# A planned attention and GEGLU kernel: one lane rule holds SP's stores, turns and loads back by a microsecond in the plan

## The chip, the cores and the metric

The kernel runs on one core of one Trainium2 chip. The metric is the device time of one execution in microseconds, the median of several executions.

Engines go by the names of the profile: PE does matmuls and PEld its weight loads, DVE, ACT and POOL do vector, activation and general work, and SP issues most of the DMA transfers. SPq and ACTq are the DMA queues that SP and ACT issue to.

## The reference

The reference is a transformer block in float32 on one sequence of 2048 tokens with 640 features: a pre-normalised attention with 32 heads of 20 features, where each token sees itself and the 255 tokens before it, and a pre-normalised GEGLU layer with 1536 hidden features, both with a residual.

```python
def _A_ref(x, wqkv, wo):
    B, S, D = x.shape
    H = 32; Dh = D // H; W = 256
    qkv = (lambda x, *d: x.transpose(*d))((x @ wqkv).reshape(B, S, 3, H, Dh), 2, 0, 3, 1, 4)
    q, k, v = qkv[0], qkv[1], qkv[2]
    scores = jnp.einsum("bhqd,bhkd->bhqk", q, k) * (Dh ** -0.5)
    idx = jnp.arange(S)
    mask = (idx[:, None] - idx[None, :] >= 0) & (idx[:, None] - idx[None, :] < W)
    scores = jnp.where(mask[None, None], scores, -1e9)
    p = _softmax(scores, axis=-1)
    o = jnp.einsum("bhqk,bhkd->bhqd", p, v)
    return (lambda x, *d: x.transpose(*d))(o, 0, 2, 1, 3).reshape(B, S, D) @ wo
def _B_ref(x, w_gate, w_up, w_down):
    return (_gelu(x @ w_gate) * (x @ w_up)) @ w_down
x = A_x
h = x + _A_ref(_layernorm(x, axis=-1), A_wqkv, A_wo)
h2 = h + _B_ref(_layernorm(h, axis=-1), B_w_gate, B_w_up, B_w_down)
```

## The kernel before

**Tiling.** Tokens go in 16 blocks of 128, two of them to a chunk of 256, so attention has eight chunks, 0 to 7. Float32 numbers are split into two float16 parts, high and low (`xh` and `xl`, `oh` and `ol`, `w1h` and `w1l` and so on), and a product is the sum of three matmuls.

**The way of a chunk.** `x_lane` loads a block of x (`load_x`, tile `xt`), normalises it to `xp` and turns it with two transposing DMAs to `xh` and `xl`. `qk(c, which)` makes the queries (`which` 0) or keys (1) of chunk c on PE; `qk_out` copies each of three pieces to a tile `qks` and ACT's queue writes it to DRAM, `qk<-qks`. In the trace's names the DRAM tile of chunk 3 is `qk30` for queries and `qk31` for keys. `stack` reads them back in the layout that the scores want, six DMAs `qT<-qk` and six DMAs `kT<-qk` on SP's queue. When both are read, `maxima` computes score tiles `ra` and `rb` (`rb<-kT,qT`) whose row maxima DVE takes (`max_out`), and the maxima are written into spare rows of `qT`. Then come the scores for the softmax (`ra<-qT,kT`), the exponentials on ACT (`pt`), the mask on POOL, and the products with the values (`pv<-pt,v`). `wo_block` multiplies the attention's output of a block (`oh`, `ol`) by `wo`, DVE adds it to the residual in `ht` (`wo_out`), and SP stores `ht` to `h_dram`. The GEGLU layer works in chunks of four blocks, loads `ht` from `h_dram`, and has the stretch behind attention to itself.

**What sets the order.** The program writes out every engine's instructions one after another, and the engines run them in that order. A planner picks that order as the program is built. The class `Clock` keeps a modelled time for each engine, for each tile's last write and read, and for DMAs a window of eight: a DMA starts in the model not before the eighth DMA ahead of it, on SP's or ACT's queue alike, has landed. The built program has the same rule, with eight semaphores that the DMAs use in turn. Every piece of work is a generator that yields what its next step needs, an engine and a time at which its inputs are ready, and `Lane` wraps it. The main loop goes through the lanes in an order of precedence, lets the first one whose `start(now)` holds take one step, and moves `now` on by 0.03 us when none does. All instructions are issued by one helper, so all have line 199 in the profile.

`start` compares the inputs' ready time with `now`: a step may start when `self.need() <= now + 0.1`. Steps that need SP alone yield `("sync",)`: the block stores to `h_dram`, the loads and turns of x, the loads of `ht`, the loads, turns and partial sums of the GEGLU layer, and also the reads in `stack` and the weights' loads in `load_lane`. Reads in `stack` of chunks from 2 on carry a pace of their own, one DMA each time that the modelled DMA line is less than `PACE` = 1.0 us ahead:

```python
if c > 1:
    yield ("sync",), lambda: nc.moved["sync"] - PACE
nc.sync.dma_start(to[rows], ...)
```

Of the kernel before, what the change touches and what calls it, by code (L numbers as in the profile page):

```python
# [253 lines left out]
def block_kernel(ctx: ExitStack, tc: tile.TileContext, x, wqkv, wo, wg, wu, wd, out):  # L254
# [27 lines left out]
    def done(name):  # L282
# [19 lines left out]
    FFBACK = dict(split_lane=0.4, scale_lane=0.4, chunk_lane=0.3, token_sums=0.1,  # L302
                  sums_lane=0.2, norm_lane=0.2)
    EARLY = 0.6
    PACE = 1.0
    SWAY = 4

# [231 lines left out]
    def products(n, term, ready=None, at_=None):  # L539


        ps = [at_[0]] if at_ else []
        col = at_[1] if at_ else 0

        def start(i):
            if ready and not ready(i) or not ps and opened["mm"] >= banks["mm"]:
                return INF
            t = nc.ready([x for ab in term(i) for x in ab], "tensor")
            return t if ps else max(t, nc.slot(psums["mm"], "mm", banks["mm"]))

        for i in range(n):
            yield ("tensor",), lambda i=i: start(i)
            if not ps:
                ps.append(bank("mm"))
            m = term(i)
            for k, (l, r) in enumerate(m):
                if k:
                    yield pe()
                o = ps[0][:, col:col + r.free_size()]
                nc.tensor.matmul(o, l, r, start=(i == 0 and k == 0),  # L560
                                 stop=(i == n - 1 and k == len(m) - 1))
                pos["dense"] += r.free_size() * 3 // len(m)
        return o
# [203 lines left out]
    def stack(c, which, d):  # L767
# [10 lines left out]
        for par in range(2):  # L778
            for m, i in enumerate(((0, 0, 1), (0, 1, 0))[which]):
                rows = slice(64 * par + DH * m, 64 * par + DH * m + DH)  # L780
                if c > 1:
                    yield ("sync",), lambda: nc.moved["sync"] - PACE
                nc.sync.dma_start(to[rows], d.rearrange("(a d i) m n -> a m d i n", a=2,
# [774 lines left out]
    class Lane:  # L1558
# [11 lines left out]
        def start(self, now):  # L1570

            if "tensor" in self.engs:
                return nc.t["tensor"] <= now + AHEAD and self.need() <= max(now, nc.t["tensor"])
            name = self.gen.__name__
            back = self.back
            if name in ("split_lane", "scale_lane"):
                back = PREP if not W["o", 0].ready else FFPREP
            elif name == "x_lane":
                back = EARLY if not B[XF].full else LATE
            elif name == "max_out" and not W["v"].ready:  # L1580
                back = RAMPMAX
            if isinstance(self.engs, Soon):
                back = max(back, OUT)
            if ffpools[1]:
                back = FFBACK.get(name, OUT)
            return (all(nc.t[e] <= now + back for e in self.engs if e != "sync")
                    and self.need() <= now + 0.1)

    load_x(0)
    load_x(1)  # L1590
# [20 lines left out]
    now = 0.0  # L1611
# [85 lines left out]
```

## Time and profile before

| | |
|---|---|
| median of three executions | 1022.89 us (1022.6 to 1025.46) |
| the profiled execution | 1022.7 us |
| its span, first to last instruction | 1020.8 us |
| mean granted clock of PE | 0.998 |
| busy: PE, PEld | 998.5 us, 698.8 us |
| busy: DVE, ACT, POOL | 748.3 us, 437.9 us, 299.4 us |
| reads `kT<-qk` and `qT<-qk` | 48 DMAs each, 160 KB |
| writes `qk<-qks` | 32 DMAs of 256 KB, 16 of 128 KB |

Times are read from one profiled execution. A row of the timeline has the start, the length, the engine, the operation with its tiles, the count of instructions that are shown as one, and in brackets the idle time of the engine in front of it with what ended it. For a DMA issue the length is that of the issue on the queue, not of the transfer; a row "DMA" in the chain has the time from issue to landing. A row of the waits has the total, the number of waits and the longest. A row of the windows has the bounds, the length, the busy time and count of PE, PEld, DVE, ACT and POOL, the granted clock, the DMA share and GB/s.

### The profile page before, as it was taken

To read this page: it belongs to the slowest core of one execution; us is meant where nothing else is said; L and a number is where in the kernel's file an instruction comes from. 1 tells how busy PE (TensorE), PEld (TensorE's weight loads), DVE (VectorE), ACT (ScalarE), POOL (GpSimd) and SP (SyncE) were. 2 spreads that over 40 slices of the span, in tenths; PEclk is the share of its full clock that TensorE was granted. 3 is DMA by queue.
4 is the path that set the end of the run, shared out by engine and by line. 5 is a ranking of instruction groups with operands and counts; after the bars stand their busy time and mean duration, and the time that the engine had idled before them with its cause. 6 is when DMAs were issued, how large, how long until landed. Compare 5 with 4: busy or idle time off the path is not lost.

```text
span 1020.8 us, 30772 instructions
## 1 busy us (share of the span) xinstructions
PE 998.5 (98%) x12925; PEld 698.8 (68%) x12925; DVE 748.3 (73%) x2221; ACT 437.9 (43%) x706; POOL 299.4 (29%) x489
## 2 busy tenths in 40 slices
PE   8999999998999999999999999989999999999998
PEld 7876677675776766776655664567777777777776
DVE  6888999885776757675688787798996975544553
ACT  6514645664445654555557643522222222221220
POOL 7102224343333432333335511254313300000000
PEclk9999999999999999999999999999999999999999
DMA  8658686271460723315303433233553532222211
GB/s 306 135 116 172 190 167 169 75 132 55 95 140 20 121 75 85 75 45 106 131 29 105 84 126 103 78 129 106 154 181 90 162 137 78 78 97 85 78 53 52
DMA packets 105835, 112.68 MB, mean 110 GB/s; under 512 B 38368, under 2 KB 79584, under 8 KB 105696
## 3 DMA queue, kind: packets, MB, share of 16 engines
q1 hardware_dynamic: 93600, 99.97, 36.4%
q10 hardware_dynamic: 12096, 10.75, 3.4%
q8 instruction: 101, 1.65, 0.7%
q14 instruction: 38, 0.31, 0.1%
HBM read 73.73 MB, written 28.84 MB: 100 GB/s over the span
## 4 chain that ended last, share of the span: by engine, by line
PE 83%; DMA 7%; DVE 5%; issue 2%; ACT 2%; SPq 1%; POOL 0%; DVEq 0%; ACTq 0%; POOLq 0%
PE mm L199 43%; PE pv L199 12%; PE ra L199 12%; PE rb L199 10%; PE tp L199 7%; DMA kT<-qk 3%; DMA qk<-qks 2%; DVE junk L199 1%; SPq L199 1%; DMA qT<-qk 1%; ACT pt L199 1%; DVE am L199 0%; DVE w1l L199 0%; DVE ht L199 0%; DMA wsl<-in_wo_dram 0%
## 5 line engine op out<-in xcount | busy, mean ns | idle before, releaser
L199 POOL TENSOR_SCALAR_AFFINE_SELECT pt<-pt 128x512 f32<-128x512 f32 x352 | 176.7, 518 | 277.5 <-ACT pt L199 261.4
L199 DVE CUSTOM_DVE_ANT_0 junk<-rb,band 128x320 bf16<-128x320 f32 x224 | 109.5, 489 | 48.5 <-PE rb L199 43.3
L199 DVE CUSTOM_DVE_ANT_0 junk<-ra,band 128x320 bf16<-128x320 f32 x224 | 109.4, 489 | 38.9 <-PE ra L199 33.4
L199 ACT ACTIVATE pt<-rb,esc 128x640 f32<-128x640 f32 (+2 forms) x129 | 98.3, 769 | 81.2 <-PE rb L199 65.5
L199 ACT ACTIVATE pt<-ra,esc 128x640 f32<-128x640 f32 (+2 forms) x127 | 96.6, 767 | 75.0 <-PE ra L199 63.9
L199 PE MATMUL pv<-pt,v 128*21 128x128 f32 x2880 | 105.3, 276 | 0.3 <-POOL pt L199 0.2
L199 PEld LDWEIGHTS <-ah 128*128 128x128 f16 x768 | 75.1, 98 | 28.4 <-issue 1.2
L199 ACT ACTIVATE gel<-gel,ffk 128x512 f32<-128x512 f32 x36 | 26.0, 722 | 144.0 <-DVE gel L199 144.0
L199 PEld LDWEIGHTS pv<-pt,v 128*21 128x21 f32 x2880 | 68.8, 100 | 10.8 <-issue 1.0
L199 PEld LDWEIGHTS <-ws 128*128 128x128 f16 x720 | 70.4, 98 | 8.2
L199 PEld LDWEIGHTS <-qT 60*64 60x64 f16 x1280 | 30.4, 104 | 66.4 <-issue 53.1
L199 PEld LDWEIGHTS <-kT 62*64 62x64 f16 x2880 | 63.5, 107 | 11.6 <-issue 8.0
L199 PEld LDWEIGHTS <-gu 128*128 128x128 f16 x440 | 42.0, 98 | 36.1 <-issue 1.7
L199 DVE SCALAR_TENSOR_TENSOR ht<-mm,ffk,ht 128x320 f32<-128x320 f32 x96 | 52.2, 545 | 12.0 <-PE mm L199 10.0
L199 ACT CAST ah<-gel 128x512 f16<-128x512 f32 x48 | 29.7, 618 | 66.7 <-DVE gel L199 64.7
L199 PE MATMUL mm<-xh,w1h 128*128 128x256 f16 x200 | 54.7, 274 | 0.9 <-DVE qks L199 0.9
L199 PE MATMUL mm<-xl,w1h 128*128 128x256 f16 x200 | 54.7, 273 | 0.0
L199 PE MATMUL mm<-xh,w1l 128*128 128x256 f16 x200 | 54.7, 273 | 0.0
L199 PE MATMUL rb<-kT,qT 60*64 60x320 f16 (+4 forms) x636 | 41.2, 283 | 9.5 <-DMA kT<-qk 8.8
L199 PE MATMUL mm<-w3h,oh 128*128 128x320 f16 x160 | 48.2, 301 | 0.0
L199 PE MATMUL mm<-w3l,oh 128*128 128x320 f16 x160 | 48.2, 301 | 0.0
L199 PE MATMUL mm<-w3h,ol 128*128 128x320 f16 x160 | 48.2, 301 | 0.0
(299 smaller groups left out, 2522.5 us busy)
## 6 DMA issues: line engine op xcount, KB each, us to landing
ws<-wsums SPq DMA_DIRECT2D x24, 640.0 KB
qk<-qks ACTq DMA_DIRECT2D x32, 256.0 KB
qT<-qk SPq DMA_DIRECT2D x48, 160.0 KB
kT<-qk SPq DMA_DIRECT2D x48, 160.0 KB
wsums<-ws SPq DMA_DIRECT2D x12, 640.0 KB
ht<-in_x_dram SPq DMA_DIRECT2D x16, 320.0 KB
h_dram<-ht SPq DMA_DIRECT2D x16, 320.0 KB
ht<-h_dram SPq DMA_DIRECT2D x16, 320.0 KB
```

The lines of the kernel that those rows point to most:

```text
L199: r = real(*args, **kw)
```

## The change

A new number `HELD` = 1.0 us is subtracted where 0.1 us was added, for steps that need SP alone, apart from those of the generators `stack` and `load_lane`. Such a step may start when its inputs have been ready for 1.0 us in the plan, and not from 0.1 us before on.

```diff
     EARLY = 0.6
+    HELD = 1.0
     PACE = 1.0
...
+            late = 0.1 if self.engs != ("sync",) or name in ("stack", "load_lane") else -HELD
             return (all(nc.t[e] <= now + back for e in self.engs if e != "sync")
-                    and self.need() <= now + 0.1)
+                    and self.need() <= now + late)
```

The planner then writes another order. On SP's queue, at the reads of chunk 3 (`qT` and `kT` from `qk30` and `qk31`; `xh`, `xl` are turns of x; the number behind a tile's name only tells its allocations apart), before:

```order
L199 DMA h_dram_72<-ht_3109 128x640
L199 DMA qT_4213<-qk30_2547 20x16x256 x5
L199 DMA ht_4264<-in_x_dram 128x640
L199 DMA_TRANSPOSE xh_4272<-xp_3336 128x5x128
L199 DMA_TRANSPOSE xl_4273<-xp_3336 128x5x128
L199 DMA xt_4319<-in_x_dram 128x640
L199 DMA qT_4213<-qk30_2547 20x16x256
L199 DMA kT_124<-qk31_2930 20x16x256 x5
L199 DMA_TRANSPOSE xh_4272<-xp_4321 128x5x128
L199 DMA_TRANSPOSE xl_4273<-xp_4321 128x5x128
L199 DMA xt_4629<-in_x_dram 128x640
L199 DMA kT_124<-qk31_2930 20x16x256
```

One turn stood between the fifth and the sixth query read, and another between the fifth and the sixth key read. The same place now:

```order
L199 DMA h_dram_72<-ht_2935 128x640
L199 DMA qT_4181<-qk30_2542 20x16x256 x6
L199 DMA kT_124<-qk31_3082 20x16x256 x3
L199 DMA_TRANSPOSE xh_4328<-xp_3170 128x5x128
L199 DMA_TRANSPOSE xl_4329<-xp_3170 128x5x128
L199 DMA xt_4401<-in_x_dram 128x640
L199 DMA kT_124<-qk31_3082 20x16x256 x3
L199 DMA ht_4523<-in_x_dram 128x640
L199 DMA_TRANSPOSE xh_4328<-xp_4403 128x5x128
L199 DMA_TRANSPOSE xl_4329<-xp_4403 128x5x128
L199 DMA xt_4651<-in_x_dram 128x640
```

The first turn has moved behind the third key read, and the second behind all twelve reads.

On SP's queue, at the reads of chunk 7 (`qk70`, `qk71`), where `ht_8519` is block 10's residual and `ht_9075` block 11's, before:

```order
L199 DMA h_dram_72<-ht_8519 128x640
L199 DMA qT_10094<-qk70_8927 20x16x256 x3
L199 DMA ht_10170<-in_x_dram 128x640
L199 DMA qT_10094<-qk70_8927 20x16x256 x3
L199 DMA kT_124<-qk71_9349 20x16x256 x6
L199 DMA h_dram_72<-ht_9075 128x640
```

All twelve reads stood behind block 10's store and ahead of block 11's. Now, with `ht_8586` for block 10 and `ht_9277` for block 11:

```order
L199 DMA h_dram_72<-ht_8586 128x640
L199 DMA ht_9967<-in_x_dram 128x640
L199 DMA qT_10028<-qk70_9131 20x16x256 x6
L199 DMA kT_124<-qk71_9797 20x16x256 x4
L199 DMA h_dram_72<-ht_9277 128x640
L199 DMA kT_124<-qk71_9797 20x16x256 x2
```

The load of the next `ht` has moved ahead of the reads, and block 11's store stands ahead of the last two key reads.

PE's order changes between about 90 and 592 us and is the same on both sides of that. At the first maximum of chunk 3, before (`w3h`, `w3l` are the parts of `wo`, with the attention's output `oh`, `ol`):

```order
L199 LDWEIGHTS oh_4416
L199 MATMUL mm_4772<-w3l_1743,oh_4416 128x320
L199 LDWEIGHTS ol_4417
L199 MATMUL mm_4772<-w3h_1742,ol_4417 128x320
L199 LDWEIGHTS qT_4213
L199 MATMUL rb_4791<-kT_124,qT_4213 64x256
```

and now (`w1h`, `w1l` are parts of the keys' weights, `pv` the product with the values):

```order
L199 MATMUL pv_125<-pt_4495,v3_122 21x128 x4
L199 MATMUL pv_125<-pt_4495,v2_121 21x128 x4
L199 MATMUL pv_125<-pt_4495,v4_123 21x128 x4
L199 LDWEIGHTS w1h_151
L199 MATMUL mm_4624<-xl_2743,w1h_151 128x256
L199 LDWEIGHTS w1l_152
L199 MATMUL mm_4624<-xh_2742,w1l_152 128x256
L199 LDWEIGHTS qT_4181
L199 MATMUL rb_4676<-kT_124,qT_4181 64x256
```

The maximum stood behind a block's `wo` product, and now it stands within the projection of the next keys, 146 rows earlier on PE.

## The prediction

> **What bounds the kernel now.** I read the page's engine row first, then the chain that ended last, the waits of PE, PE's busy time by stretch, and the timelines of PE and of the DMA issues at the places where PE stood still.
>
> ```profile
> PE 998.5 (98%) x12925; PEld 698.8 (68%) x12925; DVE 748.3 (73%) x2221; ACT 437.9 (43%) x706; POOL 299.4 (29%) x489
> PE 83%; DMA 7%; DVE 5%; issue 2%; ACT 2%; SPq 1%; POOL 0%; DVEq 0%; ACTq 0%; POOLq 0%
> PE rb L199 <- DMA kT<-qk: 8.8, 4, 4.7
> ```
>
> PE is busy for 998.5 us of a span of 1020.8, so no order of the same work can save more than the 22.3 us in which it is idle, besides time at a lower clock. The third row is the largest wait of PE: four times, 8.8 us in all, a score-maximum matmul (`rb`) waits for the last read of a chunk's keys from DRAM (`kT<-qk`). The windows say in which part of the span PE is idle (the first two figures behind the bounds are the length and PE's busy time):
>
> ```profile
> 0.00:95.00 95.00, 89.22 (x974) 71.19 (x974) 72.62 (x270) 42.45 (x89) 24.78 (x41) 1.00 0.70 180
> 95.00:592.00 497.00, 486.48 (x8955) 333.68 (x8952) 377.32 (x1330) 286.90 (x452) 189.67 (x370) 1.00 0.43 101
> 592.00:1020.80 428.80, 422.78 (x3003) 293.93 (x3001) 298.38 (x623) 108.56 (x167) 84.92 (x78) 1.00 0.32 106
> ```
>
> The order of PE's instructions is the same before and after the change up to about 90 us and again from 592 us to the end; in the 497 us between, PE has 10.5 us of idle time. Those are the stakes. The timeline of PE names 8.8 of them (start, length, what, and in brackets the idle time before it):
>
> ```profile
> 232.58 0.32 PE L199 MATMUL rb<-kT,qT 60*64 60x256 f16 x5
> 237.61 0.32 PE L199 MATMUL rb<-kT,qT 60*64 60x64 f16 x3 [4.71 <-DMA kT<-qk]
> 296.90 0.32 PE L199 MATMUL rb<-kT,qT 60*64 60x320 f16 x1
> 297.46 0.33 PE L199 MATMUL rb<-kT,qT 60*64 60x320 f16 x3 [0.24 <-DMA kT<-qk]
> 364.81 0.32 PE L199 MATMUL rb<-kT,qT 60*64 60x320 f16 x1
> 366.76 0.33 PE L199 MATMUL rb<-kT,qT 60*64 60x320 f16 x3 [1.62 <-DMA kT<-qk]
> 482.05 0.32 PE L199 MATMUL rb<-kT,qT 60*64 60x320 f16 x1
> 484.61 0.33 PE L199 MATMUL rb<-kT,qT 60*64 60x320 f16 x3 [2.24 <-DMA kT<-qk]
> 236.00:238.00 2.00, 0.39 (x15) 0.39 (x15) 0.04 (x1) 0.00 (x0) 0.00 (x0) 0.91 0.15 43
> 238.00:240.00 2.00, 2.00 (x36) 1.16 (x28) 0.96 (x4) 0.80 (x1) 0.84 (x3) 0.50 0.00 0
> 240.00:242.00 2.00, 2.00 (x47) 1.23 (x46) 1.41 (x6) 0.68 (x1) 0.58 (x1) 0.73 0.02 8
> 475.00:500.00 25.00, 22.76 (x433) 15.02 (x429) 13.98 (x55) 11.64 (x19) 8.53 (x18) 1.00 0.37 85
> ```
>
> These are chunks 3, 4, 5 and 7 of eight. From the start of the held group to its continuation pass 5.03, 0.56, 1.95 and 2.56 us, where without a wait some 0.1 would, so the four cost 9.7 us. The longest costs again: after it the granted clock is 0.50 for 2 us and 0.73 for the next 2, a loss of 1.0 + 0.54 us, call it 1.5. After the 2.24 us gap the clock stays at 1.00. Together **11.2 us** hang on late key reads.
>
> **Why the reads are late.** The DMA issues of SP and, last two rows, of ACT:
>
> ```profile
> 213.42 0.79 SPq L199 DMA_DIRECT2D qT<-qk  x1
> 214.25 11.19 SPq L199 DMA_DIRECT2D kT<-qk  x5
> 230.35 1.30 SPq L199 DMA_TRANSPOSE xh<-xp  x1
> 231.76 1.22 SPq L199 DMA_TRANSPOSE xl<-xp  x1
> 233.03 0.57 SPq L199 DMA_DIRECT2D xt<-in_x_dram  x1
> 233.66 0.77 SPq L199 DMA_DIRECT2D kT<-qk  x1
> 463.43 0.33 SPq L199 DMA_DIRECT2D h_dram<-ht  x1
> 463.93 2.35 SPq L199 DMA_DIRECT2D qT<-qk  x3
> 216.77 0.37 ACTq L199 DMA_DIRECT2D qk<-qks  x1
> 354.79 0.37 ACTq L199 DMA_DIRECT2D qk<-qks  x1
> SPq L199 <- DMA qk<-qks: 12.2, 2, 7.3
> SPq L199 <- DMA qk<-qks: 7.3, 1, 7.3
> SPq L199 <- DVE ht L199: 34.2, 1, 34.2
> 233.66 3.91 DMA kT<-qk
> 279.61 5.74 DMA qk<-qks
> 290.72 6.61 DMA kT<-qk
> 354.79 6.99 DMA qk<-qks
> 362.58 4.04 DMA kT<-qk
> 468.47 8.47 DMA qT<-qk
> 476.96 7.61 DMA kT<-qk
> ```
>
> Two causes. **Steps in front:** in chunk 3 five key reads are out by 225.4, then an x turn (`xh`, `xl`) and an x load hold the queue until 233.6, and the sixth, issued at 233.66, lands 3.91 us later: PE's 4.71 us. In chunk 7 the store `h_dram` waits 34.2 us for DVE's `ht` (the waits of SP in 455 to 490 us) and goes out at 463.43; twelve reads stand behind it. **Landings of writes:** all DMAs take turns on eight places (the planner's `window` of eight), and one waits for the landing of the eighth before it. The first wait row is SP's of 200 to 240 us, two waits with 7.3 us the longest, the second that of 340 to 370, one of 7.3 us, both for writes `qk<-qks`. The second is the one ACT issued at 354.79, which landed 6.99 us later; the key read behind it took 4.04 us (the chain's rows: issue, time to landing). That is chunk 5. The change acts on the first cause and not on the second.
>
> **The change part by part.** It adds no instruction and takes none; PE's order has as many rows as before. It asks 1.1 us more lateness of SP's stores, turns and loads, so the plan, rerun with that, puts reads ahead of them, and all engines' orders between 90 and 592 us shift with it. PE's sum over its order, each matmul timed as in the trace, stays within 0.2 us, so I cost the work itself at nothing and count waits.
>
> *Chunk 7.* `wo` of blocks 10 and 11 moves 12 to 15 us forward on PE. Counted along PE's order, block 10's store then finds `ht` ready near 440 us, and reads start near 445 where they started at 463.93. Block 11's store now stands ahead of the last two key reads; its `ht` is ready near 462 by the order. The last read lands near 469, and PE reaches the maximum near 472: no wait, 2.46 gone. If block 11's `ht` were over 3 us later, the wait would begin to return.
>
> *Chunk 3.* The order has three key reads, one turn and load, three reads, and the second turn behind all. But PE reaches the first maximum 73 matmuls earlier: 8.3 us with the matmuls timed by kind, so at 232.58 − 8.3 = 224.3 (all times on the clock of before, waits taken out). The fifth read waits for the landing of the write issued at 216.77, which stands eight DMAs ahead of it. Before, the second read waited 7.3 us for that write: 214.25 + 0.8 for the first issue + 7.3 puts the landing at 222.4, 5.6 us after its issue (the 5.74 and 6.99 rows are near). Then 0.8 to the sixth issue and 3.9 to land: 227.1. Wait 2.8 where it was 4.9. Between gaps of 2.24 and 4.71 us the rows leave open where the clock falls; 2.8 is nearest to 2.24, so I take no loss, and put the point at 3. If it fell, 1.5 more: 1018 us.
>
> By the Trainium skill, "TensorE: Matmul & The Clock Gate", section "Part 1: The HAM clock gate", the clock falls to half after an idle window of about 3.4 us, and the window runs free of the kernel. A gap of 2.8 us can't fill one, so by that rule the time would be 1016.5 and not 1018. The trace agrees as far as it goes: 0.50 after 4.71 us, 1.00 after 2.24.
>
> *Chunk 5.* Six query reads, a turn, six key reads, a turn. PE gets there some 14 us earlier, at 350.8; the fifth key read waits for a write issued at 340.3. With 6.99 to land, 0.8 to the next issue and 4.04 to land, the last read is there at 352.1: wait 1.3 where it was 1.85.
>
> *Chunk 4.* One turn and a split one now stand among the query reads instead of one among each; the key reads wait for writes as before. I take 0.8 (0 to 1.5) where it was 0.46. *Chunk 6* had no wait; I take 0.2. *Chunk 2* has none in either.
>
> *The turns themselves*, now later, feed the projections. None of these is among PE's larger waits before, and by the order they keep at least the room they had, since the projection that needs them has moved back behind the maxima: nothing, or at worst what the smallest key wait cost, 0.5 us. *The loads and stores of the tail* keep their order.
>
> Waits left: 2.8 + 0.8 + 1.3 + 0.2 = 5.1 of 11.2. Gain 6.1 us. The profiled execution took 1022.7 us (span 1020.8 and 1.9 outside), 0.2 below the median 1022.89: 1022.7 − 6.1 = 1016.6, rounded to **1016.5 us**.
>
> All hangs on L, the time of the write's landing plus the last read's: chunk 3 waits L − 6.7 (and 1.5 more for the clock if that is over 3), chunk 5 L − 9.7. I took 9.5 and 11.0 from the rows nearest by.
>
> A rule against the change: the Trainium skill, "DMA: Bandwidth & Descriptors", section "Issuing engines are not separate DMA queues", says that transfers from SP and ACT share the same 16 DMA engines and interleave, so a changed queue makes no bytes faster. The trace agrees, 3.91 us for a lone read and 8.47 for one of a heap. By it alone the reads, now twelve nearly together, would land later than I take; the rival with a large L prices that from rows.
>
> **The rivals.**
>
> *All key waits go (0.14).* The writes land sooner, or the maxima come later than I count. For it: chunk 6 has the same order of reads and no wait. Against: the 7.3 us wait for a write. 1022.7 − 11.2 = 1011.5 us; with the 1.7 us of other idle time in the stretch about 1010.
>
> *The writes hold the reads, not the turns (0.14).* For it, SP's waits for `qk<-qks`. The gain is zero where the waits left are 11.2 too: with 1.0 for chunks 4 and 6 and the clock's 1.5, 2L − 14.9 = 10.2, so L = 12.5. The same time results if the plan does not do what it says because DVE's `ht` comes late again in chunk 7 and the turns feed late. 1022 to 1023 us.
>
> *Slower (0.17).* The reads go out as a heap behind a late write: the write lands after 8 us instead of 5.6, the last read after 6.61 (the row at 290.72) instead of 3.91, L = 14.6. Chunk 3 waits 7.9 and loses 1.5 to the clock, chunk 5 waits 4.9, chunk 4 perhaps 2.0 and chunk 6 0.2: 16.5 against 11.2, 1028 us. It is over 0.3% slower from 11.2 + 3.1 = 14.3 us of waits, with L near 13.5. For it: 8.47 and 7.61 in chunk 7's heap. Against: chunks 3 and 5 themselves showed 3.91 and 4.04.
>
> **How the numbers follow.** The forecast (0.55) holds about 1013 to 1019.6. A measurement of this kernel can tell some 0.3% (3.1 us) from no change: faster is below 1019.8, slower above 1025.9. Forecast and first rival make faster 0.69; the second is same 0.14; the third is slower 0.17. The range leaves out the third alone and ends below where all waits and the other idle time are gone, above just over the second: 1010 to 1023.5.
>
> **What would show it.** Right: PE's wait for `kT<-qk` falls from 8.8 to about 5 us, no 0.50 clock near 238, none at chunk 7, the store of block 10 goes out near 440, and the largest wait left is chunk 3's. Wrong: a gap over 3 us at chunk 3 with a lowered clock, SP's store in chunk 7 again waiting for `ht` past 455, or PE waiting on another engine, DVE above all, between 95 and 592 us.

## The result

| | before | after |
|---|---|---|
| median of 8 executions | 1023.99 us (1021.04 to 1029.42) | 1018.83 us (1016.09 to 1021.89) |
| span of the profiled execution | 1020.8 us | 1016.8 us |

The ratio is 0.9942 with a 95% interval of 0.9922 to 0.9963. By the ratio the kernel is faster by about 5.9 us (the two medians differ by 5.2), where 6.4 was forecast against the median known then (1016.5 against 1022.89), and both the range and the direction held.

Where the time came from stands in the same views as for the kernel before. First the page's engine row and chain, and PE's largest waits for DMAs:

```profile
PE 998.0 (98%) x12925; PEld 699.2 (69%) x12925; DVE 756.9 (74%) x2221; ACT 436.3 (43%) x706; POOL 299.0 (29%) x489
PE 86%; DVE 7%; DMA 4%; issue 2%; ACT 1%; SPq 0%; POOL 0%; DVEq 0%; ACTq 0%
PE rb L199 <- DMA kT<-qk: 3.5, 2, 2.7
PE ra L199 <- DMA kT<-qk: 1.6, 1, 1.6
```

PE does the same work (998.0 us where it was 998.5), and DMA's share of the chain falls from 7% to 4%. The key reads cost PE 3.5 + 1.6 = 5.1 us of waiting instead of 8.8. The timeline of PE in the changed kernel shows each of these waits and two new ones:

```profile
96.54 0.27 PE L199 MATMUL mm<-xl,w0h 128*128 128x256 f16 x1 [0.57 <-DMA xl<-xp]
136.25 0.43 PE L199 MATMUL rb<-qT,kT 62*64 62x128 f16 x12 [0.67 <-DVE ht L199]
228.23 0.25 PE L199 MATMUL rb<-kT,qT 60*64 60x64 f16 x3 [2.75 <-DMA kT<-qk]
295.05 0.33 PE L199 MATMUL rb<-kT,qT 60*64 60x320 f16 x3 [0.78 <-DMA kT<-qk]
357.30 0.33 PE L199 MATMUL ra<-kT,qT 60*64 60x320 f16 x3 [1.60 <-DMA kT<-qk]
```

Chunks 3, 4 and 5 wait 2.75, 0.78 and 1.60 us; chunks 6 and 7 don't wait. The windows, with the length, PE's busy time and, third from the end, the granted clock:

```profile
95.00:592.00 497.00, 489.40 (x8983) 336.42 (x8979) 386.43 (x1338) 286.21 (x451) 188.91 (x370) 1.00 0.44 102
230.00:232.00 2.00, 2.00 (x38) 1.11 (x34) 0.44 (x4) 1.02 (x2) 0.55 (x1) 0.50 0.45 153
232.00:234.00 2.00, 2.00 (x25) 1.08 (x17) 1.67 (x7) 0.94 (x2) 0.76 (x2) 0.69 0.00 0
475.00:500.00 25.00, 25.00 (x556) 17.03 (x552) 13.41 (x51) 16.07 (x25) 9.91 (x21) 1.00 0.40 123
```

PE's idle time in the stretch is 7.6 us where it was 10.5. Chunk 7's window, with 22.76 us busy before, is now full. But the clock still fell to 0.50 behind chunk 3's shorter gap. Last, the chain's DMA rows at chunks 3 and 5 (issue, time to landing), and SP at chunk 7 with its wait there:

```profile
217.80 3.84 DMA qk<-qks
222.44 5.66 DMA kT<-qk
346.37 5.53 DMA qk<-qks
352.70 4.46 DMA kT<-qk
447.92 0.33 SPq L199 DMA_DIRECT2D h_dram<-ht  x1
451.97 4.71 SPq L199 DMA_DIRECT2D qT<-qk  x6
465.40 3.10 SPq L199 DMA_DIRECT2D kT<-qk  x4
SPq L199 <- DMA qk<-qks: 8.6, 1, 8.6
```

At chunks 3 and 5 the last key reads stand behind the landing of a write from ACT, as forecast.

### The profile page after: what moved, and what is told of

Same layout as the page of the kernel before. It is cut to its first block, busy times and chain, and to the rows that moved or that the text cites. A ratio compares the mean times of both kernels' runs of the same rounds, so it can differ in the third digit from the quotient of the medians.

```text
span 1016.8 us, 30764 instructions
## 1 busy us (share of the span) xinstructions
PE 998.0 (98%) x12925; PEld 699.2 (69%) x12925; DVE 756.9 (74%) x2221; ACT 436.3 (43%) x706; POOL 299.0 (29%) x489
## 3 DMA queue, kind: packets, MB, share of 16 engines
q8 instruction: 101, 1.65, 0.7%
## 4 chain that ended last, share of the span: by engine, by line
PE 86%; DVE 7%; DMA 4%; issue 2%; ACT 1%; SPq 0%; POOL 0%; DVEq 0%; ACTq 0%
PE mm L199 44%; PE pv L199 13%; PE ra L199 12%; PE rb L199 10%; PE tp L199 7%; DVE junk L199 2%; DMA kT<-qk 2%; DMA qk<-qks 1%; DVE am L199 1%; DMA xl<-xp 1%; DMA qT<-in_wqkv_dram 1%; SPq L199 0%; DVE qks L199 0%; DVE ht L199 0%; ACT w1h L199 0%
## 5 line engine op out<-in xcount | busy, mean ns | idle before, releaser
L199 DVE CUSTOM_DVE_ANT_0 junk<-ra,band 128x320 bf16<-128x320 f32 x240 | 117.3, 489 | 47.7 <-PE ra L199 42.8
L199 ACT ACTIVATE pt<-rb,esc 128x640 f32<-128x640 f32 (+2 forms) x138 | 104.3, 764 | 79.5 <-PE rb L199 70.1
L199 DVE CUSTOM_DVE_ANT_0 junk<-rb,band 128x320 bf16<-128x320 f32 x208 | 101.8, 490 | 37.8 <-PE rb L199 32.7
L199 ACT ACTIVATE pt<-ra,esc 128x640 f32<-128x640 f32 (+2 forms) x118 | 90.5, 772 | 78.8 <-PE ra L199 60.7
L199 PE MATMUL mm<-xl,w0h 128*128 128x256 f16 x175 | 47.9, 274 | 0.6 <-DMA xl<-xp 0.6
```

The costliest lines, as they stand in the source:

```text
L199: r = real(*args, **kw)
```

## The experiments

My theory was that the gain is made on SP's queue: chunk 3's sixth key read no longer stands behind an x turn, and chunk 7's reads no longer behind a store. What is left would be reads that wait for one of the eight places until a write from ACT has landed. Against it stood that the gain comes from PE's other order, or that the reads are late for the bytes in flight whatever their place. In the experiments that move a DMA, the plan is kept as it is, and only the moment at which a DMA is written into the program is put off, so PE, DVE and POOL keep their order. The edit is a list of (queue, first, last, behind which DMA of SP), numbered along each queue; where an entry names no queue, it is SP's, and the call has no `op`:

```diff
-            r = real(*args, **kw)
+            r = self.put(op, real, args, kw)   # held back if in LATER, written out after its SP DMA
```

The rows of these kernels have line 200 or 205 to 209 where the others have 199. Each profile below is of one execution.

### The two places on the queue alone, in the kernel before

Chunk 3's second turn with its x load, behind the sixth key read:

```diff
+    LATER = [(127,129,130)]
```

> The kernel before, with one move on SP's queue: at chunk 3 the second x turn and its x load go behind the sixth key read. All other engines keep the order of before. Theory (the gain is made on SP's queue, by what stands in front of a read): the sixth read is issued near 226 right behind the fifth, lands by about 231, PE's 4.71 us wait at 232.6 and the half clock behind it go; the waits of chunks 5 and 7 (1.6 and 2.2) stay; 6 us faster than before, ratio 0.994. Rival (the gain needs PE's other order): within 1 us of before. Rival (a landing of a write holds the sixth read in the turn's place): the wait only shrinks to 1 to 2 us, 3 to 5 us faster.

Measured: ratio 0.9939 (0.9917 to 0.9961), as much as the whole change. PE at chunks 3 and 5, and the chain at chunk 3:

```profile
234.25 0.25 PE L200 MATMUL rb<-kT,qT 60*64 60x64 f16 x3 [0.37 <-DMA kT<-qk]
362.10 0.33 PE L200 MATMUL rb<-kT,qT 60*64 60x320 f16 x3 [1.39 <-DMA kT<-qk]
226.19 4.04 DMA qk<-qks
230.24 3.96 DMA kT<-qk
```

PE's 4.71 us are 0.37, with no order but SP's changed, so PE's other order is not needed for the gain. My timing was off: the sixth read was issued at 230.24 and not near 226, since moving forward past three DMAs put it eight behind the write issued at 226.19. It still came just in time.

That place had been the turn's. In the kernel before, ACT issued the same write at 224.84, and SP waited for it from the fifth read to the turn (the issue, and SP's waits in 226 to 232 us):

```profile
224.84 0.37 ACTq L199 DMA_DIRECT2D qk<-qks  x1
SPq L199 <- DMA qk<-qks: 4.8, 1, 4.8
```

So of the 8.2 us between the fifth read and the sixth, 4.8 were a landing that holds whichever DMA has the place, and only the rest was the turn's and the x load's own. The sixth read goes out 3.4 us earlier (230.24 against 233.66), and PE reached the maximum 1.0 us later in this execution (233.56 against 232.58); together that is the difference of the two waits. Nor did chunk 7's wait stay at 2.2 us as expected: it was 0.76, with the store where it was, since the last read landed 19.6 us behind the store's issue and not 21.1. I have no run that says why.

Block 10's store and the next load behind chunk 7's reads:

```diff
+    LATER = [(191,191,204),(195,195,204)]
```

> The kernel before, with one move on SP's queue: at chunk 7 block 10's store and the load of the next ht go behind the twelve reads. Theory: the reads no longer wait for DVE's ht (34.2 us before); the key reads still wait for the last writes of keys, issued at 457.3, so they are issued near 462 and the last lands near 470 to 472; PE's 2.24 us wait at 482 goes; 2.5 us faster, ratio 0.9976. Rival (the reads are held by writes, not by the store): the wait stays over 1.5 us and the time within 1 us of before. Rival (the gain needs PE's order, with wo of block 10 earlier): the same.

Measured: ratio 0.9986 (0.9966 to 1.0007), between theory and rival and not told from either by the time alone. The profile says more: the windows of chunks 3 and 7, PE at chunk 3, and SP's wait from 440 to 466 us:

```profile
225.00:250.00 25.00, 19.44 (x377) 13.15 (x375) 13.20 (x51) 10.11 (x17) 9.00 (x19) 0.86 0.41 91
475.00:500.00 25.00, 24.44 (x483) 16.21 (x484) 15.30 (x60) 12.84 (x19) 8.49 (x18) 1.00 0.33 93
238.78 0.32 PE L200 MATMUL rb<-kT,qT 60*64 60x64 f16 x3 [5.56 <-DMA kT<-qk]
SPq L205 <- PE ra L200: 24.1, 1, 24.1
```

Chunk 7's wait for keys is gone (24.44 us busy, 22.76 before). But with the store out of the way SP waits 24.1 us for PE's scores, which still read the `qT` that the new reads overwrite, and the reads start at 461.37 where it was 463.93. Of the 34.2 us that SP's row of waits put on the store, only a few were its own. This run's chunk 3, which the edit doesn't touch, waited 5.56 us at a clock of 0.86 and hid part of the gain.

Both moves together:

```diff
+    LATER = [("sync", 127, 129, 130), ("sync", 191, 191, 204), ("sync", 195, 195, 204)]
```

> The kernel before with both moves on SP's queue: chunk 3's second turn behind the sixth key read, and block 10's store with the next load behind chunk 7's reads. If the two add up as run apart (0.9939 and 0.9986): ratio 0.9925, PE's waits for key reads at chunks 3 and 7 both under 1 us, and chunk 5's 1.4 us left. If the reads of chunk 7 only look held by the store: no better than the first move alone, 0.994.

Measured: ratio 0.9921 (0.9901 to 0.9941), near the sum, though the interval just reaches the first move alone, so the time doesn't show that the second adds to it. In the profile chunk 7 has no wait left. Chunk 3 waited 0.94 us and chunk 5 1.44; a new wait of 1.39 us for `qT<-mT`, the maxima's way into `qT`, stood at 269.7.

### One place put back, in the changed kernel

The sixth key read behind the second turn again:

```diff
+    LATER = [(126,126,130)]
```

> The changed kernel, with one move on SP's queue: at chunk 3 the sixth key read goes behind the second turn and its x load, as it stood before. Theory: the read is issued near 227.5 instead of 223, lands near 231.5, and PE's wait in chunk 3 grows from 2.75 to about 6 us with the clock as low as in the changed kernel or a little longer: 3.5 us slower than the changed kernel, so about 2 us faster than before, ratio 0.998. Rival (PE's order made the gain): as fast as the changed kernel, ratio 0.994.

Measured: ratio 1.0012 (0.9993 to 1.0031): the whole gain is gone, and more than I priced. The chain at chunk 3, PE there, and the window:

```profile
226.88 4.57 DMA kT<-qk
231.49 0.32 PE L200 MATMUL rb<-kT,qT 60*64 60x64 f16 x3 [6.95 <-DMA kT<-qk]
225.00:250.00 25.00, 18.51 (x321) 12.23 (x322) 13.25 (x55) 8.37 (x13) 5.90 (x12) 0.86 0.29 71
```

The read lands at 231.5 as expected, and PE's wait is 6.95 us. What I missed is the clock: 0.86 over the window and not 0.93 as in the changed kernel, so twice the loss at half clock. This execution was the slowest of the twelve, but the others show it too: the mean granted clock of the twelve is 0.995, against 0.998 in the changed kernel's eight.

### Whose place waits for the write, in the changed kernel

Chunk 3's first turn and its x load, behind the sixth key read:

```diff
+    LATER = [(121,123,126)]
```

> The changed kernel, with one move on SP's queue: at chunk 3 the first turn and its x load, which stand between the third and the fourth key read, go behind the sixth. Theory with landings: the last key reads then stand eight places behind query reads and not behind the write of keys that is issued at 217.8, so all are issued by about 213 and land by 220; PE's 2.75 us wait and the 1.6 us of half clock behind it go; 4.3 us faster than the changed kernel, ratio to before 0.990. Rival (the reads are late for the bytes in flight, not for a place): the wait shrinks by under 1 us, ratio 0.994. Rival (the turn is needed in time): a new PE wait for xh or xl of over 1 us.

Measured: ratio 0.9995 (0.9975 to 1.0016), by the ratios 5 us slower than the changed kernel. It is none of the three outcomes. In order: SP's issue of the turn, SP's longest wait for a write, ACT's wait in 210 to 232 us, and PE:

```profile
222.47 1.20 SPq L208 DMA_TRANSPOSE xl<-xp  x1
SPq L208 <- DMA qk<-qks: 6.0, 1, 6.0
ACT xp L200 <- DMA xl<-xp: 6.0, 1, 6.0
227.78 1.04 PE L200 MATMUL tp<-ident,oT 117*128 117x117 f32 x4 [4.76 <-ACT oT L200]
```

PE no longer waits for chunk 3's keys. But the place behind the write is now the `xl` turn's. It goes out at 222.47, ACT's cast into the single `xp` buffer waits 6.0 us for it to land, and behind the cast on ACT stands the copy `oT` that PE's transposes need: 4.76 us. A late landing has to be waited for by some DMA; what it costs depends on which.

So the next kernels deal out the places. In chunk 3 ACT's write takes its place behind the first key read, and only the x load goes behind the sixth:

```diff
+    LATER = [("scalar", 37, 37, 118), ("sync", 123, 123, 126)]
```

> The changed kernel, where at chunk 3 the places of the eight are dealt out otherwise: the write of keys that ACT issues near 217.8 takes its place behind the first key read (ACT's order: one exponential earlier than the write), and the x load goes behind the sixth key read, so no key read stands eight behind the write; the x load does. The turn stays where it is, so ACT's cast to xp is not held as it was when the turn took that place. Theory (a place held by a late write): all key reads out by 215, PE's 2.75 us wait gone and the half clock behind it; 4.3 us faster than the changed kernel, ratio to before 0.990. Rival (bytes in flight, or PE meets the next wait at once): under 1.5 us of it are gained, ratio 0.993 or more.

Measured: ratio 0.9941 (0.9921 to 0.9962), level with the changed kernel. PE at chunk 3, and a window behind it:

```profile
227.94 0.45 PE L200 MATMUL ra<-qT,kT 62*64 62x128 f16 x12 [1.72 <-DVE mxs L200]
228.00:230.00 2.00, 2.00 (x38) 1.20 (x37) 1.88 (x9) 0.79 (x1) 0.00 (x0) 0.51 0.83 258
```

Chunk 3's wait for keys went as the theory had it, but a wait of 1.72 us for DVE came in its stead (`mxs`, the maxima's end). In this execution, the slowest of six, the clock fell there and once more at chunk 5, where PE waited 2.10 us. The time is the rival's, and its second reason holds: PE met the next wait at once.

In chunk 5 nothing but a place: ACT's write takes its place behind the first turn.

```diff
+    LATER = [("scalar", 54, 54, 168)]
```

> The changed kernel, where only a place is dealt out otherwise: at chunk 5 the write of queries that ACT issues near 346.4 takes its place behind the first turn, one exponential later in ACT's order; SP's order is unchanged. The fifth and sixth key reads then stand eight behind the turn, and the second turn behind the write. Theory: the key reads are out by 349 and land by 353, PE's 1.60 us wait at chunk 5 goes; 1.6 us faster than the changed kernel, ratio to before 0.9926. Rival (the reads are late for the turn or the bytes in flight): the wait keeps over 1 us.

Measured: ratio 0.9924 (0.9897 to 0.9950), as forecast, but the interval holds the changed kernel's 0.9942 too, so the wait and not the time is what shows it. PE at chunks 3 and 5, and the windows that hold them:

```profile
226.79 0.25 PE L200 MATMUL rb<-kT,qT 60*64 60x64 f16 x3 [2.81 <-DMA kT<-qk]
351.83 0.33 PE L200 MATMUL ra<-kT,qT 60*64 60x320 f16 x3 [0.43 <-DMA qk<-qks]
225.00:250.00 25.00, 23.21 (x441) 15.88 (x445) 18.78 (x71) 12.11 (x20) 8.29 (x18) 1.00 0.33 80
```

With SP's order untouched, chunk 5's 1.60 us are 0.43: the reads were late for a place. Part of what this execution gains is chance: behind chunk 3's gap of 2.81 us, as long as the changed kernel's 2.75, the clock stayed at 1.00.

Both:

```diff
+    LATER = [("scalar", 37, 37, 118), ("sync", 123, 123, 126), ("scalar", 54, 54, 168)]
```

> The changed kernel with the places of chunk 3 and of chunk 5 both dealt out as in the two runs before. Theory: both waits go, 4.3 + 1.6 us, ratio to before 0.9885, about 1011.5 us; PE's waits for key reads are then chunk 4's 0.8 us alone. Rival: 0.993.

Measured: ratio 0.9908 (0.9890 to 0.9926), 1014.69 us, the lowest median of all the kernels, faster than the kernel before and, with intervals that only touch, than the changed one; from the chunk 5 run it can't be told apart. No wait for key reads of 0.4 us or more is left in its profile. At chunk 3 PE waits 1.00 us for DVE, and at 136.2 us 1.20 for `qT<-mT`; I had priced neither, and by the ratio the kernel is 2.3 us short of my figure.

### Which steps' lateness makes the plan

The lateness for `x_lane` alone:

```diff
-            late = 0.1 if self.engs != ("sync",) or name in ("stack", "load_lane") else -HELD
+            late = -HELD if self.engs == ("sync",) and name == "x_lane" else 0.1
```

> The kernel before with the lateness of 1.0 us for SP's steps of x_lane alone (the loads and turns of x); stores, ht loads and the GEGLU layer's steps keep 0.1 us ahead. The plan comes out almost as with the whole change: in chunk 3 three key reads, a turn, two key reads, one ht load, the sixth; in chunk 7 block 11's store behind the third key read. Theory (the turns make the gain): PE's chunk 3 wait 2.7 to 3.3 us, chunk 5's 1.6, none at chunk 7, ratio 0.994 as with the whole change. Rival (the stores' lateness carries it): 0.997 or more.

Measured: ratio 0.9936 (0.9920 to 0.9952), the whole gain. PE's waits were 1.68 us at chunk 3 and 2.77 at chunk 5, none at chunk 7; the clock fell behind both (0.93 over either window of 25 us).

For the stores to `h_dram` and the loads of `ht` from x alone:

```diff
-            late = 0.1 if self.engs != ("sync",) or name in ("stack", "load_lane") else -HELD
+            late = -HELD if self.engs == ("sync",) and name in ("wo_out", "residual") else 0.1
```

> The kernel before with the lateness for SP's stores of ht to h_dram and its loads of ht from x alone. In the plan chunk 3's reads stay split by the two turns as before; in chunk 7 the store of block 10 goes behind the fourth query read, an ht load behind the second key read. Theory: PE's chunk 3 wait of 4 to 5.5 us with the half clock stays, chunk 5's too, chunk 7's 2.2 us shrinks by up to its whole; 0 to 2.3 us faster, ratio 0.998 to 1.000. Rival: 0.994.

Measured: ratio 1.0006 (0.9988 to 1.0024). Chunk 3 waited 5.32 us and chunk 5 1.56; chunk 7's wait was gone, and small waits for DVE's `ht` (0.64 us at 488.7 the largest) took its place. The lateness of the turns is the part that pays.

### The clock behind a gap, by itself

```diff
+    for rep in range(7):
+        for k in range(10):
+            ...
+            for i in range(150):
+                tc.nc.tensor.matmul(ps[:, 0:128], g16 if i == 0 else ident16, ident16,
+                                    start=True, stop=True)
+            tc.nc.vector.tensor_copy(wide_, ps[:, 0:64])
+            for i in range(2 * k):
+                tc.nc.vector.tensor_scalar(wide_, wide_, 0.5, None, op0=ALU.mult)
+            tc.nc.vector.tensor_copy(g16[:, 0:64], wide_)
```

> The changed kernel with a measurement behind its end, whose time is not to be compared: 70 bursts of 150 float16 matmuls of 128 columns, each held by a chain of DVE copies of growing length, so PE idles from about 0.7 to 3.5 us in ten steps, seven times each. If the clock falls by a fixed length of idle time, one length parts the gaps that are followed by a clock of 0.50 from those that aren't. If it falls by the busy share of a window that runs free, gaps between some 1.4 and 3 us are followed by a fall in some repetitions and not in others, the longer the more often.

Three gaps of the timeline, and the second of the three microseconds behind each in the windows:

```profile
1059.60 0.23 PE L1663 MATMUL mm<-ident,g 128*128 128x128 f16 x1 [1.93 <-DVE g L1668]
1178.69 0.23 PE L1663 MATMUL mm<-ident,g 128*128 128x128 f16 x1 [1.93 <-DVE g L1668]
1093.77 0.29 PE L1663 MATMUL mm<-ident,g 128*128 128x128 f16 x1 [3.30 <-DVE g L1668]
1060.70:1061.70 1.00, 1.00 (x22) 1.00 (x20) 0.00 (x0) 0.00 (x0) 0.00 (x0) 1.00 0.00 0
1179.79:1180.79 1.00, 1.00 (x12) 1.00 (x11) 0.00 (x0) 0.00 (x0) 0.00 (x0) 0.50 0.08 16
1094.87:1095.87 1.00, 1.00 (x12) 1.00 (x10) 0.00 (x0) 0.00 (x0) 0.00 (x0) 0.50 0.00 0
```

The same gap of 1.93 us is followed once by full and once by half clock. Counted over all 70 gaps of this one execution, by windows of 1 us behind each:

| gap, us | 0.55 to 1.47 | 1.93 | 2.38 | 2.84 | 3.30 and 3.76 | 4.21 to 4.67 |
|---|---|---|---|---|---|---|
| gaps followed by a fall | 0 of 22 | 4 of 7 | 2 of 7 | 4 of 7 | 14 of 14 | 13 of 13 |
| full-speed time lost by one | 0 | 1.7 | 1.7 | 1.7 | 1.5 to 1.7 | 1.4 to 2.9 |

So it is no fixed length: between 1.93 and 2.84 us a gap lowers the clock or not by when it comes. The trace's clock records show what decides. All 41 stretches of half clock in this run start on one grid with steps of 3.413 us. The 29 gaps that put at most 1.89 us of idle time into any one step of it were followed by no fall, the 33 that put 2.07 us or more into one all by a fall, and the eight between, from 1.93 to 1.99 us, by four.

In the profiled executions of the kernels that have more than one fall, the falls lie on such a grid too, with a phase of its own in each. The changed kernel's gap of 2.75 us put 1.83 us into one step and the clock fell. The 2.81 us of the run that dealt out chunk 5's place were cut into 1.36 and 1.45 (by the phase of its one fall, at 1013.8 us) and it did not fall, nor did it behind the 2.24 us of the kernel before, cut into 1.04 and 1.20. In the attention stretch the edge is lower than in the bursts: gaps of 1.48 us (the sixth read put back, chunk 5), 1.65, 1.68 and 1.72 us that lay whole in one step were followed by a fall, and one of 1.62 (the kernel before, chunk 5) was not. Why is open.

The counts agree with the free-running window of the Trainium skill ("TensorE: Matmul & The Clock Gate", section "Part 1: The HAM clock gate") and with its length, since 1.7 us lost is 3.4 us at half speed. They do not agree with a whole idle window being needed.

## Why the prediction was right

**What bounds it and where it goes: right.** The waits left were forecast as 2.8, 0.8, 1.3 and 0.2 us at chunks 3 to 6 and none at chunk 7; they were 2.75, 0.78, 1.60, 0 and 0. L, the landing of the write plus that of the last read, was 3.84 + 5.66 = 9.5 at chunk 3 where I took 5.6 + 3.9: the sum held, but each half was off by 1.8 us the other way, so a wait so near the forecast is luck. So is chunk 5's: L was 5.53 + 4.46 = 10.0 where I took 11.0, and PE came 9.3 us behind the write's issue where I took 10.5. Chunk 4's 0.8 was a guess to begin with.

**Two causes, one removed: right, shown by runs, but I sized the first too large.** The turn moved alone gives 0.9939, the read put back behind the turn gives 1.0012, and a write's place dealt out otherwise takes chunk 5's wait from 1.60 to 0.43 us. But I read the whole time from 225.4 to 233.6 as the turn's. It was the turn's own wait for a landing, 4.8 us, and then 3.4: the two causes stood one behind the other in the same place.

**The clock at chunk 3: the step that failed.** I took no loss below a gap of 3 us and gave 1018 us as the price if it fell. It fell in the profiled execution behind 2.75 us. By the 70 gaps and the grid that hangs at this length on where the gap falls, which no plan sets, so the term was neither 0 nor 1.5 us but something between. The gap of 2.24 us that I leaned on had been cut by the grid. The rule of the Trainium skill ("TensorE: Matmul & The Clock Gate", section "Part 1: The HAM clock gate") that I set against it, by which a gap of 2.8 us can't fill a window, gave the same wrong zero.

**The turns at nothing, at worst 0.5 us: low.** A later turn cost PE 0.57 us at 96.5, and another new wait of 0.67 us for `ht` stood at 136.3. These 1.2 us and the clock make up most of what the profiled execution is short of the forecast; its span fell by 4.0 us, of which 0.7 had been gained by 93 us, where the order is still the same.

**The size: near, and in part by luck.** The profiled pair differs by 4.0 us and the medians by 5.2, and the granted clocks on record fit that: the profiled execution of the kernel before lost less to the clock than most. Its granted clock of 0.998 is the highest that any of 58 later executions of that kernel shows; their mean is 0.996, about 4 us of half clock lost in each (an estimate, one less the clock times the span), against about 2 us in the eight of the changed kernel. So some 2 us of the gain is clock, and some 3 is waiting, where I took 1.5 and 4.6.

**Chunk 7 by the store: right in the end, wrong in the middle.** The store went out at 447.92, which I had near 440, and the reads started at 451.97. But the key reads then waited 8.6 us for a write and came out at 465.40. The store was hardly the holder: with it moved away in the kernel before, the reads waited 24.1 us for PE's scores. Chunk 7 has no wait left in the profile of the change (the window is full), but the 34.2 us row was not its size, and in the run with the turn moved alone the wait was 0.76 us with the store in its old place.

**The rivals.** The slower one needed L of 13.5; 9.5 and 10.0 were measured. "All key waits go" did not happen; the kernel that dealt out the places as well comes near it, at 0.9908. "The writes hold the reads" holds for what is left.

## What to carry to other kernels

When a wait names a read, look at what stands in front of the read on its queue and then at which earlier transfer it has to see landed; the second can hide in the time for which the first seems to hold the queue. A late landing is paid by whichever transfer has the place behind it, so give that place to one for which nobody waits: here an x load and not a key read or a turn. And the longest wait in a queue's list is not the sum to be gained: ask what the next instruction would have waited for in its stead. Last, look at the granted clock of all executions before taking one profile for the kernel.

## What the hardware showed that I had not expected

In bursts of back-to-back matmuls the granted clock fell behind gaps as short as 1.93 us, in 10 of the 21 gaps from 1.93 to 2.84 us, and each fall at these lengths cost 1.7 us. What counted was the idle time within one step of a grid of 3.413 us, with the edge between 1.89 and 2.07 us. In the kernels the clock fell behind 2.75 us in one and not behind 2.81 in another with the same order at that place, and behind gaps down to 1.48 us that lay whole in one step. By the bursts' counts a stall of 1.9 to 2.8 us costs 0.8 us more on average (an estimate, 10 of 21 times 1.7), and executions of one order can differ by a whole fall.
